# A Fourier and token-mixing layer on one core: the order of the first loads changed

## The chip, the cores and the metric

The kernel runs on one core of one Trainium2 chip. The metric is device time of one execution in microseconds (us); the number given for a kernel is the median of its runs. Five engines work beside each other: TensorE (PE, with its weight loads shown apart as PEld), VectorE (DVE), ScalarE (ACT), GpSimd (POOL) and SyncE (SP). SyncE, ScalarE and GpSimd issue the transfers between the device's memory and the on-chip memory; each of the three has a queue of its own for them.

## The reference

The input `x` has 2048 rows of 640 values. It is normalized along its rows, and three terms are added: `x` itself, the real part of a two-dimensional Fourier transform of the normalized rows, and a two-layer network that mixes along the 2048 rows.

```python
x = A_x
xn = _layernorm(x, axis=-1)
return x + _A_ref(xn, A_dft_seq_re, A_dft_seq_im, A_dft_hid_re, A_dft_hid_im) + _B_ref(xn, B_w1, B_b1, B_w2, B_b2)
...
# _A_ref
a = jnp.einsum("bsd,ed->bse", x, dft_hid_re)
b = jnp.einsum("bsd,ed->bse", x, dft_hid_im)
y = jnp.einsum("ts,bse->bte", dft_seq_re, a) - jnp.einsum("ts,bse->bte", dft_seq_im, b)
...
# _B_ref
h = _layernorm(x, axis=-1)
u = jnp.einsum("bsd,sf->bdf", h, w1) + b1
u = _gelu(u)
y = jnp.einsum("bdf,fs->bds", u, w2) + b2
```

All inputs and the output are float32.

## The kernel before

Rows are taken in 16 blocks of 128, called rows 0 to 15 here; a block is one tile of 128 partitions by 640 values. Each operand of a product is split into a rounded high part ("hi") and the remainder ("lo"), and three products (hi by hi, hi by lo, lo by hi) are added in PSUM. Larger products are put together from fewer block products by sums and differences, in the manner of Strassen and Winograd; this concerns the stages behind the one looked at here.

The whole order of instructions is written out by hand. A list of steps is made first; each step is one piece of a matrix, with a "top" (cast the piece to its hi part, on ScalarE), a "bottom" (subtract to get the lo part, on VectorE) and the products. Then a loop walks over the steps from number 6 on (`turn_of`), issuing loads ahead. The first steps, numbers 0 to 9, are the ones in `first_columns`, and a text, `START`, gives the order in which their parts and everything around them are put into the engines' instruction streams. Each word of `START` is a letter and numbers:

- `x k`: load row `k` (`row`, L535 to L539). `b i`: load piece `i` of the sequence transform, 128x512 values (`load`, L499 to L501), into slot `FIRST_AT[i]` of the buffer `pieces`.
- `W`: a one-column activation that brings ScalarE's function table for the reciprocal root (L582).
- `M k`, `A k`: statistics of row `k` in two halves of 320 columns, and their aggregate, on VectorE (L227, L230). `R k`: the reciprocal root on ScalarE (L236), which gives `near`. `E`, `v`, `V`: the refinement of that factor, on GpSimd.
- `D0-n`: normalized columns of row 0 from `near`, on VectorE (L394); `H k`: the same for another row, on ScalarE (L288). `n`, `N`: the row normalized in place by the refined factor. `L k`: the lo part of the normalized row (L153).
- `T i`: the hi part of piece `i` (L150). For piece 0 it is in two halves: `T0-0` casts the second half on VectorE (L203), `T0-1` the first on ScalarE (L150). `B i`: the lo part (L153).
- `P i-n`: the products of piece `i` in pass `n` (L513). The first words of this kind are `P0-0 P1-0 P0-1 P1-1 P0-2 P1-2`: five matmuls of piece 0 with row 0's hi part, three of piece 1 with the same, then the two with the lo parts. Row 1's products come behind these 24.

Loads are in the order of the words on their queue. Row 0 is loaded in halves of 320 columns: the second is issued by ScalarE at the very start (L135), the first by SyncE as the first word (`x0`, L537). SyncE then issues piece 0, piece 1, row 1, piece 2, row 4, and so on. An instruction that touches a tile another instruction wrote waits for it; these waits are put in by the framework.

Before the first real product TensorE runs `WARM` matmuls on a constant (L145 to L147), ten of 512 columns and five of 128.

Of the kernel before, what the change touches and what calls it, by code (L numbers as in the profile page):

```python
# [16 lines left out]
D = 640  # L17
# [9 lines left out]
NC = S // CH  # L27
H2 = D // 2
EPS = 1e-5
AHEAD = 2  # L30
LOADS = 4
WARM = 15

BLOCK = 10
APART = 2
# [9 lines left out]
FIRST_AT = [0, 6, 1, 7, 2, 3, 4, 5, 6, 7]  # L45
# [1 line left out]


START = """
    x0 W0 b0 b1 x1 b2 x4 b3 x5 b4 x2 x3 b5 x6 x7 b6 b7  # L50
    M0 A0 T0-0 T0-1 E0 R0 D0-0 D0-1 D0-2 D0-3 v0 T1 B0 n0 B1 T2 L0 M1 A1 R1 e1 O1 H1-0-2 H1-2-5 w1 P0-0 P1-0 P0-1 P1-1 P0-2 P1-2 B2 M4-0 n1 L1-0-2 M4-1
    A4 E4 T3 R4 L1-2-5 O4 V4 H4 T4 B3 M5 A5 E5 R5 N4 O5 V5 B4 P2
    L4 P3 H5 T5 M2 A2 N5 M3 A3 R2-3 B5 F2-3 L5 q4 P4
    H2 T6 N2 M6 A6 B6 L2 q5 P5 T7 M7 B7 A7
# [23 lines left out]
def fnet_plus_mixer(  # L78
# [30 lines left out]
    nc = tc.nc  # L109
# [18 lines left out]
    x_rows = [x[t * P : (t + 1) * P, :] for t in range(NS)]  # L128
# [3 lines left out]
        keep.tile([P, 7, D], F32, name="x0", tag="slab4"), keep.tile([P, 1, D], F32, name="x1", tag="slab5"),  # L132
    ]
    x_in = [x_slab[k // 7][:, k % 7, :] for k in range(8)]
    nc.scalar.dma_start(x_in[0][:, H2:], x_rows[0][:, H2:])  # L135
    part_up = [dram.tile([P, 2, D], F32, name=f"up{r}") for r in range(NF2)]
    y_part = [[dram.tile([P, ND, CH], F32, name=f"y{m}{c}") for c in range(NC)] for m in range(2)]

# [5 lines left out]
    idle = nc.const_aps.tensor(1.0, [P, CH], dtype=BF16)  # L144
    for i in range(WARM):  # L145
        n = CH if i < WARM - 5 else P
        nc.tensor.matmul(psum[7][:, :n], idle[:, :P], idle[:, :n], start=True, stop=True)  # L147
# [34 lines left out]
    def cut_piece(source, n, tail=False, stacked=False):  # L182

        held = {}

        def of_tail():
            hi, src = (t.rearrange("p (q c) -> p q c", c=P) for t in (held["piece"][:, 0, :n], source()))
            return hi[:, :, :TAIL], hi[:, :, P - TAIL :], src[:, :, :TAIL]  # L190

        def top(part=None):
            if part:
                return high(held["piece"][:, 0, : n // 2], source()[:, : n // 2])
            cut_turn[0] = (cut_turn[0] + 1) % (AHEAD + 1)
            held["piece"] = keep.tile([P, 2, D], R32, name="piece", tag=f"cut{cut_turn[0]}")
            if tail:
                hi, _, src = of_tail()
                high(hi, src)
            elif part is None:  # L200
                high(held["piece"][:, 0, :n], source())
            else:
                nc.vector.tensor_copy(held["piece"][:, 0, n // 2 : n], source()[:, n // 2 :])  # L203

        def bottom():
            if tail:
                hi, lo, src = of_tail()
                low(lo, src, hi)
                return held["piece"][:, 0, :n], None
            hi, lo = (held["piece"][:, i, :n] for i in range(2))  # L210
            if stacked:
                last = slice(n - P, n)
                low(hi[TAIL:, last], source()[TAIL:, last], hi[TAIL:, last])
            whole = n - P if stacked else n
            low(lo[:, :whole], source()[:, :whole], hi[:, :whole])
            return hi, lo

        return top, bottom
# [13 lines left out]
    def root(var, q=None):  # L232

        if q is None:
            q = small.tile([P, NS], F32, name="q")[:, : var.shape[-1]]
        nc.scalar.activation(q, var, AF.Abs_reciprocal_sqrt, bias=eps)  # L236
        return var, q
# [25 lines left out]
    def offset(to, ks):  # L263
        nc.vector.scalar_tensor_tensor(to[:, 1, ks], mv[:, ks, 0], -1.0, to[:, 0, ks], op0=ALU.mult, op1=ALU.mult)
# [134 lines left out]
    def channels(k, j):  # L399

        a = fixed[0][k % 4]
        i = (0, 0, 6, 6)[j] if k < 4 and j < 4 else (1, 1, 2, 2)[j] if j < 4 else None
        if i is None:
            return fifth(a, 0, k // 4), fifth(a, 1, k // 4)
        at = at_slot[i] + j % 2 * P
        return a[:, 0, at : at + P], a[:, 1, at : at + P]
# [74 lines left out]
    def c_tile():  # L481

        i = c_turn[0] = (c_turn[0] + 1) % 6
        return c_place[i // 3][:, i % 3, :]

    def store_y(add, m, c, j, t):
        if not add:
            nc.gpsimd.dma_start(y_part[m][c][:, j, :], t)
        else:
            nc.gpsimd.dma_start(y_part[m][c][:, j, :], t, accum_op=ALU.add)  # L490

    def first_columns():


        raw = pieces[1].rearrange("p a q c -> p (a q) c")
        banks = {}
        vq = {}

        def load(i):  # L499
            m, k = FIRST[i][:2]  # L500
            nc.sync.dma_start(raw[:, FIRST_AT[i], :], dft_seq[m * NC, k])  # L501

        def products(w, m, k, j0, j1, passes=(0, 1, 2)):


            late_begin = 4
            js = (range(3), range(3, 5)) if (m, k) == (1, late_begin) else (range(j0, j1),)
            for n, j in ((n, j) for part in js for n in passes for j in part):
                rows, cols = ((0, 0), (0, 1), (1, 0))[n]
                begin, end = (late_begin, 1) if m == 1 and j >= 3 else (0, 5)  # L510
                if n == 0 and k == begin:
                    banks[m, j] = psum[(5 * m + j) % 8]
                nc.tensor.matmul(  # L513
                    banks[m, j], channels(k, j)[rows], w[cols], start=n == 0 and k == begin,
                    stop=n == 2 and k == end, skip_group_check=True,
                )

        def read(m, js):
            for j in js:
                c = c_tile()  # L520
                nc.scalar.activation(c, banks[m, j], AF.Copy)
                store_y(False, m, 0, j, c)

        for i, (m, k, j0, j1) in enumerate(FIRST):
            steps.append(
                cut_piece(lambda i=i: raw[:, FIRST_AT[i], :], CH)
                + (lambda w, *passes, at=(m, k, j0, j1): products(w, *at, *passes),)
            )
        reads[6].append(lambda: read(0, range(ND)))

        extras[11].append(lambda: read(1, range(2)))
        extras[12].append(lambda: read(1, range(2, 4)))
        extras[13].append(lambda: read(1, range(4, ND)))

        def row(k):  # L535
            if k == 0:
                nc.sync.dma_start(x_in[0][:, :H2], x_rows[0][:, :H2])  # L537
            else:
                nc.sync.dma_start(x_in[k], x_rows[k])  # L539

        def begin_loads(i):
            for f in loads.pop(i):
                f()

        def top(i, *part):
            steps[i][0](*part)

        def bottom(i):
            ready[i] = steps[i][1]()

        def run(i, *passes):
            steps[i][2](ready[i], passes or (0, 1, 2))
            if not passes or 2 in passes:
                del ready[i]

        def rooted(k, to=None, by=1):
            ks = slice(k, (to or k) + 1, by)
            vq[k] = root(mv[:, ks, 1], near[:, 0, ks])

        def inverted(k, to=None, by=1):  # L560
            inverse(norm[:, 0, slice(k, (to or k) + 1, by)], *vq[k])

        def factored(k, to=None, by=1):
            inverted(k, to, by)
            offset(norm, slice(k, (to or k) + 1, by))

        def whole_row(k, by_vector=False):
            if not by_vector and k not in LAST_ROWS:
                return normalize(k, x_in[k], norm)

            nc.vector.tensor_scalar(
                x_in[k], x_in[k], mv[:, k, 0:1], norm[:, 0, k : k + 1], op0=ALU.subtract, op1=ALU.mult
            )

        return {
            "x": row, "b": load, "q": begin_loads, "T": top, "B": bottom, "P": run,
            "M": lambda k, *halves: statistics(k, x_in[k], *halves), "A": aggregate,
            "R": rooted, "F": factored, "O": lambda k: offset(near, slice(k, k + 1)), "E": half_beside, "V": factors_beside, "v": lambda k: factors_beside(k, False), "n": lambda k: whole_row(k, True), "e": lambda k: half_beside(k, nc.vector), "w": lambda k: factors_beside(k, False, nc.vector),
            "D": first_hi,
            "H": lambda k, *ends: first_rows(k, 0, *ends), "N": whole_row,  # L580
            "L": lambda k, *ends: first_rows(k, 1, *ends),
            "W": lambda k: nc.scalar.activation(one, one, AF.Abs_reciprocal_sqrt),  # L582
        }
# [662 lines left out]
    with tc.manual_schedule():  # L1246
        for word in START.split():
            start[word[0]](*map(int, word[1:].split("-")))
        for i in range(FIRST_STEP, len(steps) + 1):
# [6 lines left out]
            elif i >= s_hid:  # L1256
                k = sum(i >= s for s in (s_up, s_up + 7 * NF2, s_down))
# [44 lines left out]
```

## Time and profile before

| | |
|---|---|
| median of 3 runs | 866.64 us (866.55 to 867.37) |
| the profiled execution's own time | 866.55 us |
| its span, first to last instruction | 864.8 us |
| TensorE busy | 860.2 us, 99% of the span |
| VectorE, ScalarE, GpSimd busy | 694.8, 523.0, 159.1 us |
| mean rate of the transfers | 179 GB/s over the span; 337 GB/s in the first fortieth |

Times in a profile count from the span's start. In a list of instructions in order of time, a row gives the start, the duration, the engine, the line, the operation, the tiles (written <- read), the shape, the count, and in brackets how long the engine had been idle before it and what ended the idle time. ACTq and SPq are the issuing of transfers by ScalarE and SyncE. In a list of waits the numbers are the total, the count and the longest. In a table by windows each engine has its busy time and, in brackets, the count of instructions that started. In a list of transfers the last number is the time from the issue to the landing.

### The profile page before, as it was taken

Reading aid. Unit: us, or ns where it says so; the run is one execution under the profiler, and the core shown is the slowest. Engines: PE = TensorE matmul, PEld = TensorE weight load, DVE = VectorE, ACT = ScalarE, POOL = GpSimd, SP = SyncE. Lnnn points to the kernel's source line nnn. Section 1 sums busy time; section 2 is a strip of 40 time slices with the busy share of each in tenths; the row PEclk is TensorE's granted clock in tenths of the full one; section 3 lists DMA queues with packets and bytes.
Section 4 is the critical chain, followed back from the end, with each engine's and each line's share of the span. In section 5 each row is a group of like instructions: output and inputs, shape, how many; then the busy total and the mean of one; then the engine's idle time right before and its main releaser. Section 6 shows DMA issues by size and latency. Waiting matters only on the chain.

```text
span 864.8 us, 13904 instructions
## 1 busy us (share of the span) xinstructions
PE 860.2 (99%) x4899; PEld 789.2 (91%) x4899; DVE 694.8 (80%) x1177; ACT 523.0 (60%) x968; POOL 159.1 (18%) x215
## 2 busy tenths in 40 slices
PE   9999999999999999999999999999999999999998
PEld 6888888888888888889999999999999999999998
DVE  7898868758767888677877788888679978887887
ACT  5765576763555555547565556676667866555654
POOL 2222131210020211122110101111322221101211
PEclk9999999999999999999999999999999999999999
DMA  9949596795482746869576756665688799766776
GB/s 337 368 102 273 180 255 226 161 296 149 96 188 29 195 105 141 207 112 196 125 166 159 163 140 192 189 175 161 143 184 181 161 232 234 182 141 126 158 169 149
DMA packets 90293, 154.44 MB, mean 179 GB/s; under 512 B 9008, under 2 KB 37424, under 8 KB 89968
## 3 DMA queue, kind: packets, MB, share of 16 engines
q0 software_dynamic: 25008, 57.52, 36.7%
q1 hardware_dynamic: 64928, 95.80, 34.0%
q8 instruction: 38, 0.62, 0.3%
q10 hardware_dynamic: 288, 0.25, 0.1%
q14 instruction: 31, 0.25, 0.1%
HBM read 99.96 MB, written 58.82 MB: 184 GB/s over the span
## 4 chain that ended last, share of the span: by engine, by line
PE 99%; DMA 0%; DVE 0%; ACT 0%; SPq 0%; issue 0%; DVEq 0%
PE psum L161 32%; PE psum L162 32%; PE psum L164 31%; PE psum L513 3%; DMA pieces<-in_dft_seq 0%; SPq L537 0%; DVE n L394 0%; DVE pair L952 0%; ACT piece L150 0%; ACT near L236 0%; DVEq L1298 0%
## 5 line engine op out<-in xcount | busy, mean ns | idle before, releaser
L153 DVE TENSOR_TENSOR piece<-pieces,piece 128x512 fp32r<-128x512 f32 (+4 forms) x496 | 326.8, 659 | 129.6 <-ACT piece L150 126.6
L150 ACT ACTIVATE piece<-pieces 128x512 fp32r<-128x512 f32 (+3 forms) x472 | 295.3, 626 | 223.7 <-PE psum L164 140.2
L161 PE MATMUL psum<-piece,n 128*128 128x512 f32 x540 | 210.1, 389 | 0.0
L162 PE MATMUL psum<-piece,n 128*128 128x512 f32 x540 | 210.1, 389 | 0.0
L164 PE MATMUL psum<-piece,n 128*128 128x512 f32 x540 | 210.1, 389 | 0.0
L162 PE MATMUL psum<-sup,piece 128*128 128x320 f32 x392 | 120.8, 309 | 0.0
L161 PE MATMUL psum<-sup,piece 128*128 128x320 f32 x392 | 120.8, 309 | 0.0
L162 PE MATMUL psum<-sdown,piece 128*128 128x320 f32 x392 | 120.8, 309 | 0.0
L161 PE MATMUL psum<-sdown,piece 128*128 128x320 f32 x392 | 120.8, 309 | 0.0
L161 PEld LDWEIGHTS psum<-piece,n 128*128 128x128 f32 x540 | 101.4, 188 | 21.2
L164 PEld LDWEIGHTS psum<-piece,n 128*128 128x128 f32 x540 | 101.3, 188 | 21.0
L162 PEld LDWEIGHTS psum<-piece,n 128*128 128x128 f32 x540 | 101.4, 188 | 20.9
L156 DVE TENSOR_TENSOR pieces<-pieces 128x512 f32<-128x512 f32 (+3 forms) x142 | 111.8, 792 | 3.0
L164 PE MATMUL psum<-sup,piece 128*128 128x320 f32 x368 | 113.7, 309 | 0.0
L164 PE MATMUL psum<-sdown,piece 128*128 128x320 f32 x368 | 113.7, 309 | 0.0
L490 POOL DMA_DIRECT2D y<-c x65 | 56.1, 900 | 255.1 <-DVE c L689 153.9
L164 PE MATMUL psum<-shid,piece 128*128 128x320 f32 x280 | 86.5, 309 | 0.0
L162 PE MATMUL psum<-shid,piece 128*128 128x320 f32 x280 | 86.5, 309 | 0.0
L161 PE MATMUL psum<-shid,piece 128*128 128x320 f32 x280 | 86.5, 309 | 0.0
L162 PEld LDWEIGHTS psum<-sup,piece 128*128 128x128 f32 x392 | 73.6, 188 | 0.0
L161 PEld LDWEIGHTS psum<-sdown,piece 128*128 128x128 f32 x392 | 73.6, 188 | 0.0
L161 PEld LDWEIGHTS psum<-sup,piece 128*128 128x128 f32 x392 | 73.6, 188 | 0.0
(132 smaller groups left out, 1106.2 us busy)
## 6 DMA issues: line engine op xcount, KB each, us to landing
pieces<-in_dft_seq SPq DMA_DIRECT2D x120, 256.0 KB, 5.3
y<-c POOLq DMA_DIRECT2D x105, 256.0 KB, 4.8
pieces<-in_w SPq DMA_DIRECT2D x88, 256.0 KB, 3.9
out<-pair POOLq DMA_DIRECT2D x38, 320.0 KB, 5.8
pieces<-y SPq DMA_DIRECT2D x32, 320.0 KB, 4.0
pieces<-in_w SPq DMA_DIRECT2D x32, 192.0 KB, 2.9
out<-in_x SPq DMA_DIRECT2D x16, 320.0 KB, 7.7
up<-pair POOLq DMA_DIRECT2D x8, 640.0 KB, 3.2
```

The costliest lines, as they stand in the source:

```text
L150: nc.scalar.activation(hi, src, AF.Copy)
L153: nc.vector.tensor_sub(lo, src, hi.bitcast(F32))
L156: nc.vector.tensor_sub(to, a, b)
L161: nc.tensor.matmul(psum, wh, mh, start=first, stop=False, skip_group_check=True)
L162: nc.tensor.matmul(psum, wh, ml, start=False, stop=last and wl is None, skip_group_check=True)
L164: nc.tensor.matmul(psum, wl, mh, start=False, stop=last, skip_group_check=True)
L490: nc.gpsimd.dma_start(y_part[m][c][:, j, :], t, accum_op=ALU.add)
L513: nc.tensor.matmul(banks[m, j], channels(k, j)[rows], w[cols], start=n == 0 and k == begin, stop=n == 2 and k == end, skip_group_check=True,)
```

## The change

- `WARM` is 14: nine warm-up matmuls of 512 columns and five of 128.
- Both halves of row 0 are issued by SyncE, one after the other, as the first two of its queue. ScalarE's issue at L135 is gone.
- Pieces 0 and 1 are issued by ScalarE. Ahead of piece 0's issue stands a memset by VectorE over the first 640 columns of the buffer `pieces`, which is piece 0's slot and the first 128 columns of the next (piece 2's). Piece 0's load writes where the memset wrote, so ScalarE waits for it. The word `W0` now follows `b0 b1`.
- Ahead of row 1's load stands a memset by VectorE over row 1's tile. The load waits for it, on SyncE.
- `R0` stands ahead of `T0-1`, so that ScalarE takes row 0's root before its half of piece 0's hi part. VectorE's order is unchanged but for the two memsets.

```diff
-WARM = 15
+WARM = 14
...
 START = """
-    x0 W0 b0 b1 x1 b2 x4 b3 x5 b4 x2 x3 b5 x6 x7 b6 b7
-    M0 A0 T0-0 T0-1 E0 R0 D0-0 D0-1 D0-2 D0-3 v0 T1 B0 n0 B1 T2 L0 M1 A1 R1 e1 O1 H1-0-2 H1-2-5 w1 P0-0 P1-0 P0-1 P1-1 P0-2 P1-2 B2 M4-0 n1 L1-0-2 M4-1
+    x0 b0 b1 W0 x1 b2 x4 b3 x5 b4 x2 x3 b5 x6 x7 b6 b7
+    M0 A0 T0-0 E0 R0 T0-1 D0-0 D0-1 D0-2 D0-3 v0 T1 B0 n0 B1 T2 L0 M1 A1 R1 e1 O1 H1-0-2 H1-2-5 w1 P0-0 P1-0 P0-1 P1-1 P0-2 P1-2 B2 M4-0 n1 L1-0-2 M4-1
...
-    nc.scalar.dma_start(x_in[0][:, H2:], x_rows[0][:, H2:])
...
         def load(i):
             m, k = FIRST[i][:2]
-            nc.sync.dma_start(raw[:, FIRST_AT[i], :], dft_seq[m * NC, k])
+            if i == 0:
+                nc.vector.memset(raw.rearrange("p n c -> p (n c)")[:, :D], 0.0)
+            (nc.scalar if i < 2 else nc.sync).dma_start(raw[:, FIRST_AT[i], :], dft_seq[m * NC, k])
...
         def row(k):
             if k == 0:
-                nc.sync.dma_start(x_in[0][:, :H2], x_rows[0][:, :H2])
+                for i in range(2):
+                    nc.sync.dma_start(x_in[0][:, i * H2 : (i + 1) * H2], x_rows[0][:, i * H2 : (i + 1) * H2])
             else:
+                if k == 1:
+                    nc.vector.memset(x_in[1], 0.0)
                 nc.sync.dma_start(x_in[k], x_rows[k])
```

## The prediction

> **What bounds the kernel now.** I read the page's header and chain first, then the chain of waits from the start, then TensorE's waits, because only time in which TensorE does not multiply can be won or lost.
>
> ```profile
> span 864.8 us, 13904 instructions
> ...
> PE 860.2 (99%) x4899; PEld 789.2 (91%) x4899; DVE 694.8 (80%) x1177; ACT 523.0 (60%) x968; POOL 159.1 (18%) x215
> ...
> PE 99%; DMA 0%; DVE 0%; ACT 0%; SPq 0%; issue 0%; DVEq 0%
> ```
> ```profile
> 0.76 0.39 SPq L537
> ...
> 1.20 3.25 DMA pieces<-in_dft_seq
> ...
> 4.48 0.32 ACT piece L150
> ...
> 4.85 0.30 ACT near L236
> ...
> 5.18 0.36 DVE n L394
> ...
> 5.58 27.70 PE psum L513 x120
> ```
> ```profile
> PE psum L147 <- PEq L1291: 0.8, 1, 0.8
> PE psum L513 <- DVE n L394: 0.6, 1, 0.6
> ```
> The last view lists every wait of TensorE in the whole run: 0.8 us before the warm-up matmuls and 0.6 us between them and the first real one at 5.58. After that there is none.
>
> ```profile
> 861.29 0.31 PE L162 MATMUL psum<-sdown,piece 128*128 128x320 f32 x1
> ```
> So the last matmul ends at 861.60, the span is 5.58 + 856.02 + 3.2 (864.8 - 861.60), and only the first term and new holes in the second can change. The edit reaches nothing behind the loads of FIRST; the end is as before. What has to be forecast is when the first real matmul starts and whether the next ones find their operands.
>
> **The change part by part.** The queues and engines of the start, as they stand now:
>
> ```profile
> 0.75 0.41 ACTq L135 DMA_DIRECT2D x<-in_x  x1
> ...
> 0.82 0.06 DVE L140 MEMSET one<- 128x1 f32 x1 [0.82 <-PEq L1291]
> ...
> 1.19 1.28 ACT L582 ACT_TABLE_LOAD   x1 [1.19 <-PEq L1291]
> 1.20 0.90 SPq L501 DMA_DIRECT2D pieces<-in_dft_seq  x2
> ...
> 2.14 0.43 SPq L539 DMA_DIRECT2D x<-in_x  x1
> ...
> 3.62 0.89 DVE L227 BATCH_NORM_STATS2 st<-x 128x6 f32<-128x320 f32 x2 [2.74 <-DMA x<-in_x]
> ...
> 4.48 0.42 ACT L150 ACTIVATE piece<-pieces 128x256 fp32r<-128x256 f32 x1 [1.79 <-DMA pieces<-in_dft_seq]
> 4.54 0.21 DVE L230 BATCH_NORM_AGGREGATE mv<-st 128x2 f32<-128x12 f32 x1
> 4.67 0.24 DVE L203 CAST piece<-pieces 128x256 fp32r<-128x256 f32 x1
> ...
> 6.06 0.63 ACT L150 ACTIVATE piece<-pieces 128x512 fp32r<-128x512 f32 x1 [0.91 <-DMA pieces<-in_dft_seq]
> ...
> 7.40 0.69 DVE L153 TENSOR_TENSOR piece<-pieces,piece 128x512 fp32r<-128x512 f32 x1
> ```
> The issues of DMA, each row of a window with a single issue in it (ScalarE's half of row 0, SyncE's half, then piece 0, piece 1, row 1, piece 2):
>
> ```profile
> x<-in_x ACTq DMA_DIRECT2D x1, 160.0 KB, 3.0
> x<-in_x SPq DMA_DIRECT2D x1, 160.0 KB, 2.8
> ```
> ```profile
> pieces<-in_dft_seq SPq DMA_DIRECT2D x1, 256.0 KB, 3.3
> ```
> ```profile
> pieces<-in_dft_seq SPq DMA_DIRECT2D x1, 256.0 KB, 4.4
> ```
> ```profile
> x<-in_x SPq DMA_DIRECT2D x1, 320.0 KB, 5.2
> ```
> ```profile
> pieces<-in_dft_seq SPq DMA_DIRECT2D x1, 256.0 KB, 5.3
> ```
> With the issue times (0.75, 0.76, 1.20, about 1.65, 2.14, 2.61) the landings are 3.75 and 3.56 for row 0, 4.5 for piece 0, 6.05 for piece 1, 7.34 for row 1, 7.91 for piece 2.
>
> *The memsets.* The nearest row is a vector memset of 128x256:
>
> ```profile
> L870 DVE MEMSET pieces<- 128x256 f32 x2 | 0.5, 272 | 0.0
> ```
> For 640 columns I bound it by 272 ns (all overhead) and 272 x 640/256 = 680 ns (all columns), and take 680, since 59 ns for one column (0.06 at L140) leaves little overhead. The first then ends at 0.88 + 0.68 = 1.56, the second at 2.24. VectorE has nothing else to do until row 0 lands (idle 2.74 us), so they cost nothing on their own engine.
>
> *Issue times.* SyncE issues row 0's halves at 0.76 and 1.20, and row 1 after the second memset, near 2.25, against 2.14; piece 2 and all behind it keep their order and move about 0.1 us. ScalarE issues piece 0 near 1.6 (before: 1.20) and piece 1 near 2.05 (before: 1.65). Behind the waiting issue on ScalarE stand the table load and L582's activation: 2.45 + 1.28 + 0.20 = 3.95. The first instruction that needs the table is the root, which cannot start before row 0's statistics at about 4.5, so 0.5 us covers them.
>
> *Row 0.* The same 320 KB go first. The first half now has the wire to itself for 0.45 us, so it lands 0 to 0.4 us before 3.56; the second ends where both ended before, about 3.75, give or take 0.3 (earlier with less beside it, later where piece 0, issued at 1.6, takes turns with it). Statistics then end near 4.25 instead of 4.51 (3.62 + 0.89), the root can start near 4.6 instead of 4.85. Range: 0.5 earlier to 0.3 later.
>
> *Piece 0 and the swap of root and hi half.* Piece 0 is issued 0.4 later but no longer stands behind row 0 in one queue, and the bytes before it are the same: 4.5 again, 4.2 to 4.8. After it the copy (0.24) and the first slice of row 0 (0.36) on VectorE, beside the hi half (0.42) on ScalarE behind the root (0.30): with the root at 4.6 the hi half runs 4.9 to 5.3, and the first matmul starts near 5.35, 0.2 earlier than 5.58. The swap by itself is worth nothing before, because the root waited for the aggregate (4.54 + 0.21 = 4.75) and began at 4.85, only 0.05 after the hi half let it. One warm-up matmul fewer: the last ends at 4.94 now, before either start, so 0.
>
> *Piece 1.* This is the term that decides. TensorE takes five products of piece 0, then three of piece 1, in program order:
>
> ```profile
> 5.58:6.95 1.37, 1.37 (x5) 1.00 0.96 339
> 5.58:6.97 1.39, 1.39 (x6) 1.00 0.96 339
> ```
> The sixth matmul started at 6.96; its hi half ended at 6.06 + 0.63 = 6.69, a slack of 0.27. Before, piece 1 stood directly behind piece 0 in SyncE's queue and ahead of row 1. Now it stands on another queue, 0.4 us later, and row 1 and piece 2 come on SyncE's at the same time. Row 0's halves, on the two queues at nearly one time, landed 0.2 us apart (3.56 and 3.75): the queues share the engines. Lower bound for piece 1: 5.75, its landing now less the 0.3 that piece 0 may gain. Upper bound: 7.9, where piece 2 landed, with everything up to it ahead. If piece 1 and row 1 share evenly, both end near the point where the same four transfers were through before, 7.34, piece 1 a little ahead as it begins about 0.2 us earlier. I take 7.0. Then the hi half ends at 7.0 + 0.03 + 0.63 = 7.66 and the sixth matmul starts at 7.68: 0.72 later than before, and an earlier first matmul gains nothing, it only waits longer.
>
> The Trainium skill, DMA: Bandwidth & Descriptors, "Queues, rings and completion order", says that each DMA engine takes turns between rings with work, a whole packet of descriptors from one before it goes to the other; by that rule an engine done with piece 0 would take its whole part of row 1 before any of piece 1, piece 1 would land near 7.3 and the sum would be 867.6. The two landings 0.2 us apart agree that queues take turns, and cannot tell how coarse the turns are.
>
> *What comes next.* Piece 1's lo half (L153 at 7.40) follows its hi half, so VectorE goes on at about 7.7, 0.3 later. Row 1's normalized columns hang on that chain:
>
> ```profile
> 10.42 1.20 ACT L288 ACTIVATE n<-x,near 128x256 fp32r<-128x256 f32 x2 [0.23 <-DVE near L264]
> ...
> 5.58:11.51 5.93, 5.93 (x26) 1.00 1.02 372
> ```
> They end at 11.62, 4.22 after L153's start at 7.40. The 27th matmul, which needs them, follows the sixth by 21 slots of (11.50 - 6.96)/20 = 0.227, 4.77. With both chains now hung on the hi half at 7.66, 0.5 us of slack stays. So the hole appears once.
>
> *Sum.* 866.55 (the profiled execution's own time, 1.75 over its span) + 0.72 = 867.27, so 867.3. The profiled execution lies 0.09 under the median of the runs.
>
> **The rivals.** (1) *Piece 1 keeps its place.* If the memsets hold row 1 long enough, or the queues do not share evenly, piece 1 lands by 6.0 or before, and the earlier row 0 counts. At 5.95 the sixth matmul may start at 6.63: a gain of 0.33, 866.2; the most is what the first matmul gains, 0.5 (866.05). For it: the second memset holds row 1 until 2.25, after piece 1's issue at 2.05. Against it: 0.2 us of lead is little beside the 1.55 us between piece 0's and piece 1's landings, and piece 0 is still under way when row 1 joins.
>
> (2) *Nothing moves.* The second half of row 0 lands as late as now or later since it is issued at 1.20 instead of 0.75, the first matmul stays at 5.6, and piece 1 comes within its 0.27 us of slack: 866.5 to 866.7.
>
> (3) *The stall costs the clock too* (the slower side). Warm-up rows show what a slow clock costs:
>
> ```profile
> 1.17 0.15 PEld L147 LDWEIGHTS <-const-bfloat16-1.0 128*128 128x128 bf16 x1 [0.27 <-issue]
> 1.60 0.15 PEld L147 LDWEIGHTS <-const-bfloat16-1.0 128*128 128x128 bf16 x1 [0.28 <-issue]
> ...
> 3.73 0.15 PEld L147 LDWEIGHTS <-const-bfloat16-1.0 128*128 128x128 bf16 x1 [0.28 <-issue]
> 4.05 0.71 PEld L147 LDWEIGHTS <-const-bfloat16-1.0 128*128 128x128 bf16 x6 [0.17 <-issue]
> ```
> A 512-column matmul took 0.43 there until about 4.0, against 0.227 later, though the clock column reads 1.00. If the hole behind the fifth matmul puts TensorE back into that state for as long as the first time (0.79 to 4.0, 3.2 us), half of it is lost: 0.72 + 1.6 = 2.3, 868.9. It decides from the point where the pause is long enough; the 0.64 us before 5.58 was not, as the pitch of 0.227 shows. Piece 1 landing behind piece 2, at 7.9 or later, gives 868.2 even without it.
>
> The Trainium skill, TensorE: Matmul & The Clock Gate, Part 1, puts the fall to half clock behind an idle window of about 3.4 us; a pause of 1 to 1.5 us would not bring it by that rule. No run here shows such a pause.
>
> **How the numbers follow.** Forecast (piece 1 shares and lands 6.5 to 7.6, time 866.75 to 867.85): 0.62. Rival 1: 0.20. Rival 2: 0.09. Rival 3 with its neighbour: 0.09. The range from 866.1 to 868.3 takes in rival 1's gain and a landing of piece 1 up to about 8.0; what lies outside is rival 3 and the scatter of single runs (866.55 to 867.37 in three). A change of 0.2%, 1.73 us, is about what a measurement can tell from none. Faster by that would need the first matmul at 3.85, before its statistics can exist: 0.02. Slower by that needs rival 3: 0.10. Within: 0.88.
>
> **What would show it.** Right: ScalarE's 128x512 activation waits for piece 1's DMA and starts near 7.0; TensorE has a second wait, of 0.7 to 1.3 us, put down to that activation, near 6.5; the first matmul starts at 5.1 to 5.6; the last ends at 862.3. Wrong: no wait of TensorE at the sixth matmul (then rival 1 or 2, told apart by the first matmul's start), matmuls of a 0.43 pitch behind it (rival 3), a first matmul after 5.9 (row 0 is disturbed by piece 0), or a new wait at row 1's matmuls.

## The result, and the profile after

| | before | after |
|---|---|---|
| median | 866.67 us (11 runs, 866.55 to 867.37) | 869.26 us (11 runs, 867.87 to 870.06) |
| ratio, with its 95% interval | | 1.0028 (1.0019 to 1.0037) |
| the profiled execution: time, span | 866.55, 864.8 | 868.17, 866.0 |
| time outside the span, over all runs | 1.72 to 1.84 (27 runs in the first series) | 2.10 to 2.18 |

The changed kernel is 2.6 us slower, and its runs lie 2.2 us apart where those before lie 0.8 apart. The forecast was 867.3 with a range up to 868.3. The profiled execution, 868.17, is one of the shorter runs, so the profile after explains 1.6 of the 2.6 us; the rest needs other executions.

From the page of the kernel after, its header and the first line of its chain:

```profile
span 866.0 us, 13906 instructions
...
PE 860.6 (99%) x4898; PEld 789.5 (91%) x4898; DVE 696.4 (80%) x1179; ACT 523.1 (60%) x968; POOL 159.0 (18%) x215
...
PE 99%; DMA 1%; DVE 0%; issue 0%; DVEq 0%
```

The chain of waits of the kernel after, in order of time (start, duration, what):

```profile
0.99 0.60 DVE pieces L501
...
1.61 4.36 DMA pieces<-in_dft_seq
...
6.00 0.29 DVE piece L202
6.29 0.27 DVE n L393
...
6.69 3.39 PE psum L514 x13
```

The chain now begins with the memset, runs through 4.36 us of piece 0's transfer, and skips row 0's statistics altogether. Before, the same piece took 3.25 us from an issue at 1.20; now it goes out at 1.61 and lands at 5.97 instead of 4.45. The first real product starts at 6.69, 1.11 us later than 5.58. TensorE's waits of the kernel after:

```profile
PE psum L514 <- DVE n L393: 1.4, 1, 1.4
PE psum L146 <- PEq L1295: 0.8, 1, 0.8
```

There is still one wait after the warm-up, 1.4 us for 0.6. What became of row 0 and of piece 1, in the timeline of the kernel after:

```profile
3.06 0.49 DVE L226 BATCH_NORM_STATS2 st<-x 128x6 f32<-128x320 f32 x1 [0.81 <-DMA x<-in_x]
...
3.86 0.49 DVE L226 BATCH_NORM_STATS2 st<-x 128x6 f32<-128x320 f32 x1 [0.30 <-DMA x<-in_x]
...
4.70 0.29 ACT L235 ACTIVATE near<-mv,eps 128x1 f32<-128x1 f32 x1 [0.69 <-DVE mv L229]
...
6.00 0.42 ACT L149 ACTIVATE piece<-pieces 128x256 fp32r<-128x256 f32 x1 [1.01 <-DMA pieces<-in_dft_seq]
...
7.28 0.63 ACT L149 ACTIVATE piece<-pieces 128x512 fp32r<-128x512 f32 x1 [0.87 <-DMA pieces<-in_dft_seq]
```

Row 0's halves do come earlier and the root runs at 4.70 for 4.85. Then ScalarE stands still for 1.01 us until piece 0 is there. Piece 1's hi part starts at 7.28 (before: 6.06) and ends at 7.91. The table by windows, of TensorE alone:

```profile
6.69:7.97 1.28, 1.28 (x5) 1.00 1.04 381
6.69:7.99 1.30, 1.30 (x6) 1.00 1.04 382
```

The sixth matmul starts at 7.98, 1.02 us later than 6.96. From there to the last matmul the two kernels agree:

```profile
862.42 0.31 PE L161 MATMUL psum<-sdown,piece 128*128 128x320 f32 x1
```

862.73 - 7.98 = 854.75 after, 861.60 - 6.96 = 854.64 before. Two chains meet at the sixth matmul of this execution. The five products ahead of it took 1.29 us from 6.69, as they do where nothing else is waited for (1.28 in e6 below). And its weight load waited for the hi part of piece 1, which ended at 7.91:

```profile
7.96 7.19 PEld L514 LDWEIGHTS psum<-piece,n 128*128 128x128 f32 x32 [0.26 <-ACT piece L149]
```

So an earlier piece 0 alone would have won almost nothing here, and an earlier piece 1 alone neither. In all, this execution lost 1.0 us ahead of the sixth matmul, 0.1 behind it, 0.1 between the last matmul and the end of the span (3.27 for 3.17), and 0.42 outside the span (868.17 - 866.0 = 2.17 for 1.75).

### The profile page after: what moved, and what is told of

Its sections match the earlier page's. It is cut to its first block, busy times and chain, and to the rows that moved or that the text cites. A ratio compares the mean times of both kernels' runs of the same rounds, so it can differ in the third digit from the quotient of the medians.

```text
span 866.0 us, 13906 instructions
## 1 busy us (share of the span) xinstructions
PE 860.6 (99%) x4898; PEld 789.5 (91%) x4898; DVE 696.4 (80%) x1179; ACT 523.1 (60%) x968; POOL 159.0 (18%) x215
## 4 chain that ended last, share of the span: by engine, by line
PE 99%; DMA 1%; DVE 0%; issue 0%; DVEq 0%
PE psum L160 32%; PE psum L161 32%; PE psum L163 31%; PE psum L514 3%; DMA pieces<-in_dft_seq 1%; DVE pieces L501 0%; DVE pair L956 0%; DVE piece L202 0%; DVE n L393 0%; DVEq L1302 0%; DVE one L139 0%
## 5 line engine op out<-in xcount | busy, mean ns | idle before, releaser
L160 PEld LDWEIGHTS psum<-sup,piece 128*128 128x128 f32 x392 | 73.6, 188 | 0.0
L160 PEld LDWEIGHTS psum<-sdown,piece 128*128 128x128 f32 x392 | 73.6, 188 | 0.0
L161 PEld LDWEIGHTS psum<-sdown,piece 128*128 128x128 f32 x392 | 73.6, 188 | 0.0
```

The source lines that it names most:

```text
L160: nc.tensor.matmul(psum, wh, mh, start=first, stop=False, skip_group_check=True)
L161: nc.tensor.matmul(psum, wh, ml, start=False, stop=last and wl is None, skip_group_check=True)
```

## The experiments

The first four ran on one chip, then e5 to e8, then e9 to e12, then e13 and e14; the kernel before ran beside each group, with medians of 866.68, 866.63, 866.60 and 866.60. "Outside" is the time of a run less its span.

| run | kernel | median (lowest to highest), runs | median span | outside |
|---|---|---|---|---|
| | after | 869.26 (867.87 to 870.06), 11 | 867.1 | 2.10 to 2.18 |
| e1 | after, again | 870.11 (867.82 to 870.60), 5 | 868.0 | 2.10 to 2.13 |
| e2 | after, 17 warm-up matmuls | 868.32 (867.22 to 868.94), 11 | 866.1 | 2.10 to 2.22 |
| e3 | after, one queue, no memsets | 867.26 (866.95 to 869.93), 11 | 865.4 | 1.77 to 1.86 |
| e4 | after, row 1 held longer | 867.76 (866.82 to 870.73), 10 | 865.65 | 2.09 to 2.16 |
| e5 | after, row 1 not held | 870.57 (869.74 to 872.52), 4 | 868.45 | 2.10 to 2.14 |
| e6 | after, one queue, both memsets | 868.04 (867.63 to 869.83), 10 | 865.85 | 2.12 to 2.23 |
| e7 | before, 14 warm-up matmuls | 866.72 (866.36 to 868.36), 11 | 864.9 | 1.72 to 1.82 |
| e8 | e3 with 17 warm-up matmuls | 867.53 (867.09 to 867.99), 11 | 865.7 | 1.79 to 1.88 |
| e9 | before, two more tiny memsets | 867.03 (866.77 to 867.72), 8 | 864.9 | 2.07 to 2.13 |
| e10 | before, row 1 held | 866.75 (866.61 to 867.12), 8 | 864.95 | 1.79 to 1.82 |
| e11 | before, 17 warm-up matmuls | 866.73 (866.36 to 867.41), 11 | 865.0 | 1.72 to 1.81 |
| e12 | piece 0 alone on ScalarE's queue | 867.36 (866.92 to 867.63), 11 | 865.3 | 2.06 to 2.18 |
| e13 | e8 with row 0 as one transfer | 867.00 (866.56 to 867.23), 11 | 865.2 | 1.77 to 1.86 |
| e14 | e8 without the swap | 867.64 (867.22 to 868.58), 11 | 865.8 | 1.72 to 1.84 |

### The clock: e1, e2, e7

e1 is the changed kernel again, unchanged.

> The changed kernel once more, beside the next three on one chip. Theory (two causes: piece 0 lands near 6.0 us beside row 1 on the other queue, and in part of the runs the clock is granted a window later): runs fall into two groups, near 868.2 with a mean granted clock of 1.000 and near 869.8 with 0.998. Rival (one cause, the landing of piece 0 scatters by 2 us): the times lie evenly between 867.9 and 870.1, and the clock does not go with them.

The granted clock is the share of its full clock that TensorE was given; of a run there is the mean over its span. The five runs: 870.60, 870.33 and 869.60 with a mean of 0.998, 870.11 with 0.999, 867.82 with 1.000. With the eleven of the result there are sixteen. Five lie below 869 us, at 0.999 or 1.000, with 868.17 in the middle. Eleven lie above, with 869.83 in the middle; seven of these have 0.998. A mean of 0.999 tells nothing: the profiled execution of e8 has it too, and there the clock falls at 863.86, behind the last matmul, which ended at 861.95. So seven runs are shown to have lost clock. The four others above 869 (one at 1.000, three at 0.999) fit a first grant that comes late, as in e5 below, but none of them was profiled. There are, roughly, the two groups. The profiled execution of e1 (870.60) shows what the upper one is. TensorE by windows (stretch, its length, busy time and count, granted clock, then the transfers):

```profile
4.28:7.69 3.41, 1.66 (x11) 1.00 1.01 366
7.69:11.11 3.42, 3.42 (x9) 0.50 1.04 393
11.11:14.52 3.41, 3.41 (x17) 1.00 1.04 402
```

In the first of these stretches TensorE was busy for 1.66 of 3.41 us: the warm-up had ended at 4.89 and the first product started at 6.64, a pause of 1.75 us. For the whole of the next stretch the clock was granted at half, and nine matmuls were started where seventeen are in the stretch after it. 3.42/2 = 1.7 us are lost, which is the distance of the two groups (869.83 - 868.17). The profiled execution of the result had a pause of 1.37 us (warm-up until 5.32, first product at 6.69), and in the same stretches kept the full clock, with 16 matmuls. The windows of its clock had other borders: its trace has the first grant at 5.61 us, that of e1 at 4.28. The two stretches in the result's execution:

```profile
4.28:7.69 3.41, 2.04 (x11) 1.00 0.98 329
7.69:11.11 3.42, 3.42 (x16) 1.00 1.04 397
```

The Trainium skill, TensorE: Matmul & The Clock Gate, Part 1, gives the window as free-running and about 3.4 us long, with the fall to half clock after an idle window. The stretch of 3.41 us agrees. The condition does not: here the clock fell after a stretch in which TensorE was busy for half of the time, and after a pause of 1.75 us. The measurement decides: a pause shorter than the window that the Trainium skill gives can cost the clock.

e2 fills the pause:

```diff
-WARM = 14
+WARM = 17
```

> The changed kernel with 17 warm-up matmuls for 14, so that they end near 6.6 us at the slow clock, where the first real product starts. Theory of two causes: no run below a mean granted clock of 1.000, median 867.9 to 868.4, spread under 0.6 us. Rival (the landing of piece 0 alone): the same median and spread as the changed kernel, 869.3 and 2 us.

No run had a clock below 1.000, none lay above 869, and the median fell by 0.94 us to 868.32 (by 1.79 against the five runs of e1 beside it). The spread stayed wide, 1.7 us where under 0.6 was expected, so the clock was one cause and not the only one. In the profiled execution piece 0 landed at 4.7, but the longer warm-up was still running, and the first product followed it at 6.35 without a wait. The sixth started at 7.71, after its weight load had waited 0.40 us for piece 1's hi part: here the forecast's own mechanism stands alone, 0.03 from its 7.68. e7 takes the warm-up matmul away from the kernel before:

```diff
-WARM = 15
+WARM = 14
```

> The kernel before with 14 warm-up matmuls for 15, nothing else. Theory (the clock is granted by windows, and the pause ahead of the first product decides): the pause grows from 0.64 to about 0.9 us; most runs 866.4 to 867.4 as before, none to three of eleven near 868.5. Rival (14 is what makes the second group of one queue at 869.1 to 869.9): about four of eleven runs near 868.5 to 869. Prediction's step: no difference at all.

The median is 866.72 against 866.63 of the runs beside it: nothing. Two of the eleven runs, 867.73 and 868.36, lie outside what the kernel before showed in its 27 runs there (up to 867.63). The pause did not grow as expected in its profiled execution: the first grant came late (6.54), the warm-up ran at the slow clock until 5.32 and the first product started at 5.43. So the fifteenth matmul is worth little where piece 0 comes early, and 0.94 us go with three more where the pause is 1.4 to 1.8.

### The queues: e3 to e6

e3 keeps row 0 in turn, the swap and 14 warm-up matmuls, and takes the rest back:

```diff
-            if i == 0:
-                nc.vector.memset(raw.rearrange("p n c -> p (n c)")[:, :D], 0.0)
-            (nc.scalar if i < 2 else nc.sync).dma_start(raw[:, FIRST_AT[i], :], dft_seq[m * NC, k])
+            nc.sync.dma_start(raw[:, FIRST_AT[i], :], dft_seq[m * NC, k])
...
-                if k == 1:
-                    nc.vector.memset(x_in[1], 0.0)
```

> The changed kernel with pieces 0 and 1 back on SyncE's queue and both memsets left out: row 0 in turn, the root ahead and 14 warm-up matmuls stay. Theory (sharing the engines with row 1 is what delays piece 0): piece 0 lands at 4.3 to 4.6 us, the first real product starts by 5.6, time 866.2 to 866.9. Rival (row 0 in turn or the root ahead costs the time): the first product stays at 6 us or later, time above 867.5.

Piece 0's cast on VectorE in e3:

```profile
4.90 0.29 DVE L202 CAST piece<-pieces 128x256 fp32r<-128x256 f32 x1 [0.68 <-DMA pieces<-in_dft_seq]
```

Piece 0 landed at 4.88, the first product started at 5.60, and seven of eleven runs lie between 866.95 and 867.43; the other four lie at 869.1 to 869.9. One of these has a mean clock of 0.998; that all four are the clock is argued from e8, which differs by three more warm-up matmuls and has none of them. The median is 2 us off the changed kernel's median, though not quite the 866.9 that was expected at most.

e4 and e5 change only when row 1, and with it all behind it, joins on SyncE's queue:

```diff
 # e4
-                    nc.vector.memset(x_in[1], 0.0)
+                    for _ in range(3):
+                        nc.gpsimd.memset(x_in[1], 0.0)
 # e5
-                if k == 1:
-                    nc.vector.memset(x_in[1], 0.0)
```

> The changed kernel with row 1 held by three memsets on GpSimd in place of one on VectorE, so that its issue (and all behind it on SyncE) comes near 4 us instead of 2.28. Theory (sharing): piece 0 lands at 4.3 to 4.7 and piece 1 by 5.8, the first product starts at 5.0 to 5.5, time 866.0 to 866.8 unless row 1 then comes too late for its statistics at 8.7. Rival (ScalarE's queue is itself slow or its issue too late): piece 0 lands at 5.5 or later as before.

> The changed kernel without the memset on row 1, so that row 1 is issued at 1.65 us and not at 2.28. Theory (pieces 0 and 1 lose to whatever shares the engines with them from SyncE's queue): piece 0 lands later still, at 6 to 7 us, where one queue for all gave 4.88 and a long hold 5.2; median 869.5 to 871. Rival (the order of issue on SyncE does not matter to ScalarE's queue): piece 0 at 4.7 to 6.0 as in the three runs of the changed order, median 868 to 870.

The same cast in e4, then in e5:

```profile
5.23 0.32 DVE L202 CAST piece<-pieces 128x256 fp32r<-128x256 f32 x1 [1.02 <-DMA pieces<-in_dft_seq]
```
```profile
7.00 0.29 DVE L202 CAST piece<-pieces 128x256 fp32r<-128x256 f32 x1 [2.69 <-DMA pieces<-in_dft_seq]
```

Row 1 issued at 3.08 us (e4; 4 was meant): piece 0 at 5.21, median 867.76. At 2.28 (the change): 5.97, 5.93 and 4.7 in three profiled executions (result, e1, e2), 869.26. At 1.66 (e5): 6.98, 870.57. The medians rise by 1.5 and 1.3 us as row 1 comes sooner, in the order that sharing predicts, but they hold the cost of the clock as well.

Piece 0's landings alone do not show sharing, since the three of one order lie 1.3 us apart. Piece 1's keep the order without overlap: its hi part, which waited for its transfer each time, started at 5.87 in e4, at 7.28, 7.55 and 7.02 in the three, and at 8.29 in e5; on one queue it started at 5.59 (e3), 6.56 (e6) and 5.95 (e8). The bytes go the same way. Between 3.6 and 4.6 us ScalarE's queue moved 0.34 MB and SyncE's next to nothing in e4, 0.17 and 0.04 in the result's execution, 0.16 and 0.11 in e1, 0.25 and 0.07 in e2, 0.12 and 0.24 in e5. The sums differ too, 0.22 to 0.36 MB, so sharing is not all that differs.

e4's landing of piece 0, 5.2, is neither the 4.7 of the theory nor the 5.5 of the rival, and its median lies 1 us above the 866.8 that the theory allowed; e5 came out as its theory has it.

In e5 the late product met the cold clock as well. TensorE by windows in e5:

```profile
7.70:12.90 5.20, 5.20 (x12) 1.00 1.01 365
12.90:16.00 3.10, 3.10 (x15) 1.00 1.03 391
```

Twelve matmuls in 5.20 us, 0.433 each, then fifteen in 3.10, 0.207: the full clock came only near 12.9, and the column says 1.00 for the slow stretch too. The trace's first record of a grant starts at 12.98, and the column takes what lies ahead of the first record as full, so a late first grant has to be read from the pitch.

e6 puts the pieces on one queue and keeps both memsets:

```diff
-            (nc.scalar if i < 2 else nc.sync).dma_start(raw[:, FIRST_AT[i], :], dft_seq[m * NC, k])
+            nc.sync.dma_start(raw[:, FIRST_AT[i], :], dft_seq[m * NC, k])
```

> The changed kernel with both memsets but with pieces 0 and 1 on SyncE's queue. Two questions. Start: with one queue, piece 0 lands at 4.7 to 5.0 and the first product starts by 5.8 if the queue is the cause; at 6 or later if the memsets are. Time outside the span: 1.72 to 1.86 us in the kernel before and with one queue, 2.09 to 2.22 in all with pieces on ScalarE's queue; 1.8 here puts those 0.35 us down to the queue, 2.1 to the memsets.

The start is undecided: piece 0 landed at 5.83 in its profiled execution, later than in e3 and e8 (4.88 and 5.26), although all three issue it at 1.66. Single landings scatter by a microsecond, so only medians can be compared: 868.04, less 0.33 outside the span, is 0.45 above e3. From the changed kernel e6 differs by the queue alone, and its median is 1.22 us lower, all of it in the span: that is the price of the second queue with 14 warm-up matmuls, its cost in clock included. The second question is answered: the 0.35 us outside the span are there without the queue.

### What is left at a steady clock: e8, e11, e13, e14

e8 is e3, e11 the kernel before, each with `WARM = 17`.

> One queue for all as before in the series, with 17 warm-up matmuls for 14. Theory (its four slow runs of eleven were the clock): all runs within 866.4 to 867.4, none near 869. Rival (they were late landings of piece 0): again a third of the runs near 869.

> The kernel before with 17 warm-up matmuls for 15. Theory (its runs up to 867.6 are those in which the clock is granted late or the pause of 0.64 us costs something): median 866.4 to 866.6 and none above 867.0. Rival (warm-up at the slow clock now ends behind 5.58 in some runs and delays the first product): a group at 866.9 to 867.4, median no better than before.

e8 has no run near 869, as the clock theory says, but starts at 867.09: its median is 0.80 above e11's. e11 is 866.73, no better than the kernel before; longer warm-up does not help where the pause is short, and its expected gain did not come. What its rival named was seen instead: in the profiled execution the first product started at 5.92 (5.58 in the kernel before), without a wait and straight behind the warm-up, though VectorE had begun row 0's columns at 5.10 (5.18 before), and four of the eleven runs lie at 866.94 to 867.41.

e13 loads row 0 by one transfer, so that piece 0 goes out second again; e14 puts the hi half back ahead of the root:

```diff
 # e13, on e8
-                for i in range(2):
-                    nc.sync.dma_start(x_in[0][:, i * H2 : (i + 1) * H2], x_rows[0][:, i * H2 : (i + 1) * H2])
+                nc.sync.dma_start(x_in[0], x_rows[0])
 # e14, on e8
-    M0 A0 T0-0 E0 R0 T0-1
+    M0 A0 T0-0 T0-1 E0 R0
```

> One queue for all with 17 warm-up matmuls, but row 0 as one transfer of 320 KB in place of two halves in turn: one issue less ahead of piece 0, which goes out near 1.2 us again and not at 1.66. Theory (the 0.8 us between this queue order with halves, 867.53, and the kernel before with 17 warm-up matmuls, 866.73, is piece 0's issue 0.46 us later): piece 0 lands at 4.3 to 4.8, row 0 near 3.6, the first product starts at 5.3 to 5.7, median 866.4 to 866.9. Rival (row 0 in front on one queue costs it, whatever the number of issues): piece 0 after 4.9, median 867.3 or more.

> One queue for all with halves in turn and 17 warm-up matmuls, with the hi half of piece 0 ahead of the root again. Theory: piece 0 lands after row 0's statistics in this order, so the root waits behind the hi half: it starts at piece 0's landing plus 0.4 in place of about 4.3 us, and the first product comes 0.3 to 0.6 later than with the swap: median 867.8 to 868.2, against 867.53. Rival (the swap is worth nothing, as the prediction has it for the kernel before): 867.3 to 867.7.

In e13 piece 0 is issued at 1.19 and lands 3.0 us later; row 0 lands whole at 3.50. Issue and landing of piece 0, then ScalarE's root and hi parts:

```profile
pieces<-in_dft_seq SPq DMA_DIRECT2D x1, 256.0 KB, 3.0
```
```profile
4.75 0.29 ACT L235 ACTIVATE near<-mv,eps 128x1 f32<-128x1 f32 x1 [2.50 <-DVE mv L229]
4.95 0.92 ACT L149 ACTIVATE piece<-pieces 128x256 fp32r<-128x256 f32 x2
```

Nothing waits for piece 0 here, and the median is 867.00: 0.53 of the 0.80 us go with issuing piece 0, and all behind it on the queue, 0.46 us later. The remaining 0.27 have no shown cause. It fell just outside both expectations, nearer to the theory's 866.9. In e14 the root does stand behind the hi half:

```profile
5.11 0.42 ACT L149 ACTIVATE piece<-pieces 128x256 fp32r<-128x256 f32 x1 [2.86 <-DMA pieces<-in_dft_seq]
5.43 0.28 ACT L235 ACTIVATE near<-mv,eps 128x1 f32<-128x1 f32 x1
```

The root started at 5.43 as expected, but the median rose by 0.11 only, within the scatter; in the profiled execution the warm-up ran on, most of it at the slow clock, the first product followed it at 6.29 without a wait, and so the later root was hidden. How much the swap is worth stays open.

### Outside the span: e9, e10

```diff
 # e9, on the kernel before
-    nc.vector.memset(one, 1.0)
+    for _ in range(3):
+        nc.vector.memset(one, 1.0)
 # e10, on the kernel before
+                if k == 1:
+                    nc.vector.memset(x_in[1], 0.0)
```

> The kernel before with two more one-column memsets of the same tile on VectorE (0.06 us each, long before its first other work). The time outside the span: 1.72 to 1.84 us if the 0.35 us come from what the memsets write or from the loads that wait for them, 2.09 to 2.22 if two more instructions on VectorE are enough. The span stays 864.6 to 865.6 in both cases.

> The kernel before with the memset on row 1 ahead of row 1's load, nothing else. Ends near 1.5 us, before SyncE comes to row 1 at 2.14, so the span does not move (864.6 to 865.6). The time outside the span: 2.1 if a memset of a tile that a load then writes is the cause, 1.8 if not.

Two one-column memsets of a tile that was set anyway put the time outside to 2.07 to 2.13, with the span where it was. The memset of 128x640 that a load waits for does not (1.79 to 1.82), and costs nothing else: 866.75. So neither the bytes written nor a load that waits is the cause; what the step does go with is in the last section.

### A try at keeping the gain: e12

```diff
-WARM = 14
+WARM = 17
...
-                nc.vector.memset(raw.rearrange("p n c -> p (n c)")[:, :D], 0.0)
-            (nc.scalar if i < 2 else nc.sync).dma_start(raw[:, FIRST_AT[i], :], dft_seq[m * NC, k])
+                nc.vector.memset(raw.rearrange("p n c -> p (n c)")[:, : D // 2], 0.0)
+            (nc.scalar if i < 1 else nc.sync).dma_start(raw[:, FIRST_AT[i], :], dft_seq[m * NC, k])
...
-                if k == 1:
-                    nc.vector.memset(x_in[1], 0.0)
```

> A try at keeping the earlier statistics: the changed kernel with piece 0 alone on ScalarE's queue behind a memset of half the size (issued near 1.35 us), piece 1 back on SyncE's queue ahead of row 1, no hold of row 1, 17 warm-up matmuls. Theory: piece 0 shares only with row 0's second half and piece 1 and lands at 4.3 to 4.9, the root runs at 4.4 to 4.7, the first product starts at 5.1 to 5.5, time 866.4 to 867.0 with the 0.35 us outside the span. Rival (any transfer on ScalarE's queue beside SyncE's lands late on some of the 16 engines): piece 0 after 5.2, time above 867.2.

Piece 0 landed at 4.68, in time, but row 0's second half now shared with it. VectorE's second half of the statistics in e12, for 3.86 in the kernel after:

```profile
4.49 0.49 DVE L226 BATCH_NORM_STATS2 st<-x 128x6 f32<-128x320 f32 x1 [0.91 <-DMA x<-in_x]
```

Row 0's columns started at 5.65 (5.18 in the kernel before), and the first product at 6.16, again straight behind the warm-up. The median is 867.36: piece 0 landed as the theory has it, the time is the rival's. No version tried beats the kernel before.

## Why the prediction was wrong

- *What bounds the kernel* was right. TensorE has no wait behind its first products in either kernel, and 854.6 to 854.8 us follow the sixth matmul in both.
- *Piece 1 and the sixth matmul* were right in mechanism and near in size: in the profiled execution a landing at 7.23 for 7.0 (issue at 2.03 and 5.2) and a sixth matmul at 7.98 for 7.68, where piece 0's chain ended too; in e2, 7.71. The second wait of TensorE that was to show it, 0.7 to 1.3 us, is not in the profile after, because the first product was late as well.

```profile
pieces<-in_dft_seq ACTq DMA_DIRECT2D x1, 256.0 KB, 5.2
```

- *Piece 0* is the step that failed. It was given 4.2 to 4.8 because "the bytes before it are the same". Sharing with row 1 was charged to piece 1 and not to piece 0, which is under way at the same time, and the 0.4 us of later issue were taken as hidden behind row 0. The first product was to start at 5.35; it started at 6.69 and 6.64 in the profiled executions of the result and of e1, after landings of 5.97 and 5.93. In e2 piece 0 landed at 4.7, so a landing near the forecast can happen in this order too. The direct cost is small where piece 1 holds the sixth matmul anyway. What it opened is the pause ahead of the first product, 1.37 and 1.75 us, and with it the loss of clock. An issue 0.46 us later was not free either: 0.53 us in e13.
- *One warm-up matmul fewer* was put at 0, since the warm-up ended at 4.94, ahead of either start. That end hangs on when the clock is granted: with 14 matmuls it was 4.89 in e1 and 5.32 in e7. In the kernel before the step holds all the same (e7, 0.09). In the changed kernel three more matmuls are worth 0.94.
- *The clock* was rival 3, with a chance of 0.09, a point of decision that was left as "long enough", and the pause looked for behind the fifth matmul. The pause that did it lies ahead of the first, where piece 0's landing put it; the price of 1.6 us was right (1.7). Seven of sixteen runs are shown to have paid it and four more probably did, so it was the likeliest case and not the tail.
- *The range* ended at 868.3 by piece 1 landing at 8.0. The measured median lies above it, 0.4 over rival 3's 868.9, since that sum had neither piece 0 nor the time outside the span in it.
- *Outside the span* was taken as fixed at 1.75 us. It is 2.10 to 2.18, and these 0.35 us are in every run of the changed kernel.
- *Row 0 and the root* went the way forecast: the root 0.15 earlier for 0.25. The memsets took 0.59 us each for 0.68 and held what they were to hold. The sum 2.45 + 1.28 + 0.20 is 3.93 and not 3.95, which changes nothing; ScalarE's activation ended at 4.00.

The forecast of 867.3 was thus short by 0.9 us for the profiled execution (0.30 at the sixth matmul, 0.42 outside the span, 0.1 behind the sixth matmul and 0.1 behind the last) and, at the median, by the clock on top. At medians the 2.6 us come apart as follows, each from two kernels that differ by it: 866.73 (e11) to 867.53 (e8), 0.80 for row 0 in turn on one queue with the swap, of which 0.53 is the later issue of piece 0 and what follows it; 867.53 to 868.32 (e2), 0.79 for the pieces on ScalarE's queue and the memsets, of which about 0.35 lie outside the span; 868.32 to 869.26, 0.94 for the clock. Each step is about as large as the interval of a single ratio reaches to either side (0.8 us), so the sizes are rough.

## What to carry to other kernels

A transfer that is put on a second queue to get ahead shares the engines with what the first queue issues meanwhile. Here the second piece on that queue could be used from 7.0 to 7.6 us on, and from 5.6 to 6.6 on with one queue in the order of need; for the first piece the landings of the two ways overlap (4.7 to 6.0 and 4.9 to 5.8). Where the bottleneck engine starts with a warm-up, look at the pause between the warm-up and the first real work before all else: a microsecond more of waiting there can cost another 1.7 through the clock. A longer warm-up shields against that, but where the clock is granted late it runs past the point at which the work could begin (6.35 in e2, 5.92 in e11). Read several executions when a profile shows less than the median does.

## What the runs showed that was not expected

**A step outside the span.** Counting all of VectorE's records in a trace, waits and branches among them, the kernels fall in two sets, without exception: 1589 or 1590 records (the kernel before, e3, e7, e8, e10, e11, e13, e14), 1.72 to 1.88 us outside the span; 1591 or 1592 (after, e1, e2, e4, e5, e6, e9, e12), 2.06 to 2.23. Neither the queues nor the memsets' sizes go with it, and two memsets of one column each are enough. What happens in these 0.33 us is not in any view, and why the step lies there was not tried.

**Half-busy is not busy enough.** The clock fell for one stretch of 3.42 us after one with 1.66 of 3.41 us busy and no pause over 1.75 us, in a kernel that is 99% busy otherwise. With stretches of that length counted from the first grant of each trace, the clock stayed after one with 2.13 us busy (e6, 5.06 to 8.48) and one with 2.33 (the result's execution, 5.61 to 9.02). So in these traces the limit lies between 1.66 and 2.13 of 3.41 us; nothing narrower was tried.

**Landings scatter.** The same order of issue, row 0 in turn and piece 0 third on SyncE's queue at 1.66, landed piece 0 at 4.88 (e3), 5.09 (e14), 5.26 (e8) and 5.83 (e6, which has the memsets besides), while the kernel before had 4.45. The changed kernel's own order gave 4.7, 5.93 and 5.97. One profiled landing does not tell two orders apart.
